# Attention and a three-way maxout layer on one core: two pairs of heads a turn, with the 64-row matmuls gathered in three stretches

## The chip, the cores and the metric

The kernel runs on one core of a Trainium2 chip. The metric is device time of one execution in microseconds (us). The kernel before takes 367.74 us, the median of three runs (367.64 to 367.95).

A core has engines that run side by side and wait for each other by semaphores. TensorE multiplies matrices; the profile calls it PE, and its weight loads PEld. VectorE is DVE, ScalarE is ACT, GpSimd is POOL. SyncE, called SP, here only issues DMAs, one after another in the order of the program. Matmul results land in PSUM, which has 8 banks, each 128 partitions wide with 512 float32 numbers per partition; everything else is in SBUF.

## The reference

```python
q, k, v: (8, 12, 448, 64) float32          # batch, heads, positions, head size
scores = matmul(q, k.transpose(0, 1, 3, 2)) / sqrt(64)
m = max(scores); e = exp(scores - m)
attn = matmul(e / (sum(e) + exp(-m) + 1e-09), v)
x = attn.transpose(0, 2, 1, 3).reshape(3584, 768)
h = maximum(maximum(x @ w1, x @ w2), x @ w3)   # weights 768 x 768
out = h @ w_out                                # 3584 x 768 float32
```

The softmax has one extra term of exp(0) in its sum. The kernel leaves the maximum out of both sides, so the sum becomes the sum of exp(scores) plus 1.

## The kernel before

**Pairs.** Heads are worked on in pairs, 6 pairs per batch, 48 in all, numbered p from 0 to 47. One iteration `it` of the loop at line 452 does the scores of pair p = it and finishes pair it - 1. A pair needs these matmuls, each 448 columns long:

- `scores(p, c)`, line 235, for three blocks c of 128 keys: two matmuls on 64 rows of the array each, one per head (line 239). They stand on different halves of the array, so that both run at once. The result fills one `ps_s` buffer of two banks; there are two such buffers.
- `scores_last(p)`, line 251: the last 64 keys of both heads in one matmul on the whole array (line 255).
- `av_main(p, hh)`, line 269, for each head: three matmuls on the whole array that sum exp(scores) times v (line 273). Columns of ones beside v give the softmax sums in the same matmul.
- `av_last(p, avs)`, line 282: two 64-row matmuls, again one per head, for the last 64 keys (line 285). Each head has one bank of `ps_av`, and there are two of them.

ACT takes the exponentials (`exp_scores`, line 249, 128 x 896 elements; `exp_last`, line 265, 128 x 448). It also makes the reciprocal of the sums as exp(-ln(sum + 1)) in `reciprocals`, lines 298 and 299. DVE multiplies by it in `normalize`, line 307, once per head.

**Dense work between.** When a batch is finished, `batch_done`, line 435, puts its maxout and output work on a list. A *group* is six matmuls into one of the two `ps_u` banks and one DVE instruction that empties it: 18 *up* groups per batch (`up_group`, lines 356, 370 and 372) and 6 or 8 *output* groups (`out_group`, lines 390 and 415). Two output groups fill one `o_sb` tile, which two DMAs on SP then write to memory (line 429). There are 6 output groups (three tiles) for even batches and 8 (four tiles) for odd ones. The pool of `o_sb` tiles, line 67, has three buffers, so every tile takes the buffer of the third tile before it, and its first write waits until both DMAs of that one have landed. `group()` takes the next group off the list. An iteration calls it three to five times, and spreads what the list holds evenly over what is left of the batch, down to `LEFT` = 4.

**Getting q and k ready.** From pair 12 on (`P_DMA`) `cast_qk(p)`, line 165, turns q and k into 16 bits on DVE, into one of two buffers. `transposes(p)`, line 209, is one DMA transpose on SP into one of three `qkT` buffers. `scale_v(p)`, line 191, prepares v on POOL. `load(p, 1)`, line 83, issues six DMAs on SP for the raw q, k and v of a pair.

**The order is written out by hand.** The pools run under a manual schedule, so each engine executes its instructions in the order in which the code emits them. From pair 12 on an iteration emits:

1. `cast_qk(it + 2)`, `transposes(it + 2)` and `scale_v(it + 1)`
2. scores and exponentials of p, blocks 0 and 1
3. one group
4. `av_main` and `av_last` of the previous pair
5. block 2 and `scores_last` of p, then reciprocals of the previous pair, then the exponentials of p
6. a group, `normalize` of head 0, a group, `normalize` of head 1, more groups
7. `load(it + 5, 1)`

So TensorE goes four times in each iteration between 64-row and whole-array matmuls: into and out of the four of step 2, and into and out of a stretch made of `av_last` and block 2.

On SP an iteration is one transpose, the output DMAs of its groups, and six loads. The code itself follows.

Of the kernel before, what the change touches and what calls it, by code (L numbers as in the profile page):

```python
# [10 lines left out]
FP32 = mybir.dt.float32  # L11
# [10 lines left out]
def kernel(  # L22
# [11 lines left out]
    nc = tc.nc  # L34
# [4 lines left out]
    NB = 3  # L39
# [125 lines left out]
    def cast_qk(p):  # L165
        qt, kt, _ = raw[(p // HB) % NRAW]
        h0 = 2 * (p % HB)
        hs = slice(h0, h0 + 2)
        k6, q6 = k16[p % NK], q16[p % NK]
        if p == 0:  # L170

            nc.scalar.copy(out=k6[:, 0:NB], in_=kt[:, hs, 0:NB].rearrange("p h c d -> p c h d"))
            for eng, cs in ((nc.scalar.copy, slice(0, 2)), (nc.vector.tensor_copy, slice(2, NB + 1))):
                eng(out=q6[:, cs], in_=qt[:, hs, cs].rearrange("p h c d -> p c h d"))
        else:
            if p >= P_DMA and (p // NPAIR) % 2:

                nc.vector.tensor_copy(
                    out=q6[:, 1 : NB + 1], in_=qt[:, hs, 0:NB].rearrange("p h c d -> p c h d")
                )  # L180
                nc.vector.tensor_copy(out=q6[64:128, 0], in_=qt[0:64, hs, NB])
            else:
                nc.vector.tensor_copy(out=q6, in_=qt[:, hs].rearrange("p h c d -> p c h d"))  # L183
            nc.vector.tensor_copy(  # L184
                out=k6[:, 0:NB], in_=kt[:, hs, 0:NB].rearrange("p h c d -> p c h d")
            )
        for hh, half in enumerate(halves):
            last = nc.gpsimd if p == 0 else nc.vector
            last.tensor_copy(out=k6[half, NB, hh], in_=kt[0:64, h0 + hh, NB])  # L189
# [14 lines left out]
    def transposes(p):  # L204
        odd = (p // NPAIR) % 2
        qkT = att_pool.tile([2 * D, 1024], MMDT, tag="qkT", bufs=3)
        qkTs[p] = qkT, 0, S
        if p >= P_DMA:
            nc.sync.dma_start_transpose(
                out=qkT.rearrange("q (c p) -> q c p", p=128),  # L210
                in_=qk16[p % NK].rearrange("p c h d -> p (c h d)"),
            )
            qkTs[p] = qkT, 64 * odd, 512
            return
        trT = ps_u.tile([128, 1024], MMDT, tag="u", name="trT")


        order = (NB, 0, 1, 2) if odd else (0, 1, 2, NB)
        n0 = 0
        for c in order:  # L220
            nc.tensor.transpose(  # L221
                out=trT[:, n0 : n0 + 128], in_=q16[p % NK][:, c], identity=ident16
            )
            n0 += SL if c == NB else 128
        for c in range(NB + 1):
            nc.tensor.transpose(  # L226
                out=trT[:, S + c * 128 : S + c * 128 + 128], in_=k16[p % NK][:, c], identity=ident16
            )
        if p == 0:
            nc.vector.tensor_copy(out=qkT[:, 0 : S + 128], in_=trT[:, 0 : S + 128])  # L230
            nc.scalar.copy(out=qkT[:, S + 128 : S + 512], in_=trT[:, S + 128 : S + 512])
        else:
            nc.vector.tensor_copy(out=qkT[:, 0 : S + 512], in_=trT[:, 0 : S + 512])  # L233
# [14 lines left out]
    def exp_scores(p, c, stp):  # L248
        nc.scalar.activation(out=eT[:, p % 2, c], in_=stp[:, :, 0:S], func=AF.Exp, scale=scale)  # L249

    def scores_last(p):
# [9 lines left out]
        )  # L261
        return stl

    def exp_last(p, stl):
        nc.scalar.activation(out=eL[:, p % 2], in_=stl[:, 0, 0:S], func=AF.Exp, scale=scale)  # L265

# [182 lines left out]
    casts(0)  # L449
    transposes(0)  # L450
    keep_busy(3)
    for it in range(NP + 1):
        p = it if it < NP else None
        prev = it - 1 if it > 0 else None
        to_next = NPAIR - it % NPAIR
        n_groups = -(-max(len(queue) - LEFT, 0) // to_next) if it % NPAIR else 4
        n_groups = max(3, min(5, n_groups))

        first = {3: 1, 4: 2}.get(it)
        if first is not None:  # L460
            hs = slice(2 * first, 2 * first + 2)
            nc.vector.memset(raw[2][0][64:128, hs, NB - 1 : NB + 1, :], 0.0)
            if first == 1:
                load(NPAIR, 1, "v")
            load(NPAIR + first, 1)
        if it in (3, 4):
            load_weight(0, it - 3)
        if it in (5, 6, 8):
            load_weight((5, 6, 8).index(it) + 1)
        if it < NPAIR:  # L470

            casts(it + 1)
            for c in range(2):
                exp_scores(p, c, scores(p, c))
            if prev is None:
                keep_busy(3)
                exp_scores(p, 2, scores(p, 2))
                transposes(1)
                exp_last(p, scores_last(p))
            else:  # L480
                den, av = (ps_av.tile([128, 512], FP32, tag="av", name=n) for n in ("den", "av"))
                sums_main(prev, den, 1)
                stp = scores(p, 2)
                sums_main(prev, av, 0)
                stl = scores_last(p)
                sums_last(prev, den, 1)
                sums_last(prev, av, 0)
                exp_scores(p, 2, stp)
                exp_last(p, stl)
                rb = reciprocals_one(den)  # L490
                transposes(it + 1)
            if it < NPAIR - 1:
                keep_busy(3)
            else:

                ups = [up_open()]
                up_part(ups[0], 0, 0, 0, range(3))
                av5 = ps_s.tile([128, 2, 512], FP32, tag="s", name="av5")
                sums_main(p, av5[:, 1], 1)
                sums_main(p, av5[:, 0], 0)  # L500
                sums_last(p, av5[:, 1], 1)
                sums_last(p, av5[:, 0], 0)
                rb5 = reciprocals_one(av5[:, 1])
            if prev is not None:
                normalize_one(prev, av, rb)
            if it == NPAIR - 1:
                normalize_one(p, av5[:, 0], rb5)
                batch_done(0)
        elif it == NPAIR:
            exp_scores(p, 0, scores(p, 0))  # L510

            up_part(ups[0], 0, 0, 0, (3,))
            ups.append(up_open())
            up_part(ups[1], 0, 0, 1, range(4))
            ups.append(up_open(ps_av, "av"))
            up_part(ups[2], 0, 0, 2, range(4))
            for dc in (4, 5):
                for fc, ps in enumerate(ups):
                    up_part(ps, 0, 0, fc, (dc,))
                    if dc == 5:  # L520
                        up_close(ps, 0, 0, fc)
            del queue[0:3]
            exp_scores(p, 1, scores(p, 1))
            group()
            casts(it + 1)
            exp_scores(p, 2, scores(p, 2))
            exp_last(p, scores_last(p))
            group()
            transposes(it + 1)
            group()  # L530
        else:
            late = it + 1 < P_DMA
            if not late:

                if it + 2 < NP:
                    cast_qk(it + 2)
                    transposes(it + 2)
                if it + 1 < NP:
                    scale_v(it + 1)
            if p is not None:  # L540
                for c in range(2):
                    exp_scores(p, c, scores(p, c))
            group()
            if late:
                casts(it + 1)
            avs = [av_main(prev, hh) for hh in range(2)]
            av_last(prev, avs)
            if p is not None:
                stp = scores(p, 2)
                stl = scores_last(p)  # L550
            rb = reciprocals(prev, avs)
            if p is not None:
                exp_scores(p, 2, stp)
                exp_last(p, stl)
            if late:
                transposes(it + 1)
            group()
            normalize(prev, 0, avs, rb)
            group()
            normalize(prev, 1, avs, rb)  # L560
            if it % NPAIR == 0:
                batch_done(prev // NPAIR)
            if it + 2 == P_DMA:
                cast_qk(it + 2)
                transposes(it + 2)
            for _ in range(n_groups - 3):
                group()

        for n in range(NPAIR + HB, 2 * NPAIR) if it == NPAIR else (it + 5,):
            if it >= NPAIR and n < NP:  # L570
                load(n, 1)
    while queue:
        group()

# [29 lines left out]
```

## Time and profile before

| | |
|---|---|
| median of 3 runs | 367.74 us |
| the profiled execution | 367.07 us |
| its span, first to last instruction | 365.3 us |
| DVE busy | 243.4 us |
| ACT busy | 221.1 us |
| POOL busy | 53.6 us |
| HBM traffic over the span | 146 GB/s |

The span is what the trace covers; about 1.8 us of the execution lie around it. In the trace a row gives start, duration, engine, source line and operation, and x6 means that six equal instructions were merged into the row. Matmuls overlap: the next one starts before the last one's duration is over, so the pace is read from starts, not from durations. A row marked SPq is a DMA's issue, and the profile tells separately how long after the start of its issue the data had landed.

### The profile page before, as it was taken

How to read it: one execution, taken by the hardware profiler on the slowest of the kernel's cores; microseconds unless marked ns; L12 is line 12 of the kernel's file. 1: busy time of each engine (PE TensorE's matmuls, PEld its weight loads, DVE VectorE, ACT ScalarE, POOL GpSimd, SP SyncE). 2: the span in 40 equal slices, each digit the busy share in tenths (PEclk: the TensorE clock that was granted, in tenths of full speed). 3: DMA queues.
4: the chain of work that ended last, by engine and by line, in shares of the span. 5: the costliest groups of instructions: out<-in, count | busy, mean ns of one | idle time of the engine just before them, and what ended most of it. 6: DMA issues, size and time to landing. Idle time of an engine off the chain costs nothing.

```text
span 365.3 us, 6122 instructions
## 1 busy us (share of the span) xinstructions
PE 357.4 (98%) x2086; PEld 163.9 (45%) x2086; DVE 243.4 (67%) x521; ACT 221.1 (61%) x335; POOL 53.6 (15%) x159
## 2 busy tenths in 40 slices
PE   8999999999999999999999999999999999999995
PEld 3434444444444444444444444444444444445552
DVE  4474777876578677577657867757666776555553
ACT  4996476765666766666567666666566766651000
POOL 4263112211211211211121121121112112000000
PEclk9999999999999999999999999999999999999999
DMA  5999997668667888849764896758675673005006
GB/s 151 229 234 229 233 247 211 155 177 214 161 180 182 208 184 154 195 107 185 182 173 122 178 200 164 175 133 214 159 174 137 165 208 83 5 2 131 2 0 172
DMA packets 87951, 58.61 MB, mean 160 GB/s; under 512 B 43504, under 2 KB 84464, under 8 KB 87920
## 3 DMA queue, kind: packets, MB, share of 16 engines
q1 hardware_dynamic: 83632, 53.18, 59.7%
q0 software_dynamic: 3920, 4.72, 7.5%
q10 hardware_dynamic: 368, 0.33, 0.4%
q8 instruction: 16, 0.26, 0.3%
q14 instruction: 15, 0.12, 0.1%
HBM read 42.47 MB, written 11.01 MB: 146 GB/s over the span
## 4 chain that ended last, share of the span: by engine, by line
PE 91%; ACT 2%; DMA 2%; DVE 2%; issue 1%; SPq 0%; DVEq 0%
PE up L356 44%; PE op L390 15%; PE av L273 13%; PE stp L239 8%; PE stl L255 4%; PE av L285 3%; DMA kin<-in_k_dram 2%; PE busy L349 2%; ACT eT L249 1%; PE trT L221 1%; PE trT L226 1%; PE av L316 1%; DVE qkT L233 1%; DVE o_sb L415 0%; DVE qk L183 0%
## 5 line engine op out<-in xcount | busy, mean ns | idle before, releaser
L356 PE MATMUL up<-xT,w 128*128 128x448 f16 x864 | 175.3, 353 | 0.7 <-DVE xT L307 0.4
L249 ACT ACTIVATE eT<-stp 128x896 f16<-128x896 f32 x144 | 125.5, 910 | 53.3 <-PE stp L239 53.3
L356 PEld LDWEIGHTS <-w 128*128 128x128 f16 x864 | 81.7, 98 | 81.7 <-issue 12.5
L372 DVE TENSOR_TENSOR hT<-hT,up 128x448 f16<-128x448 f16 x96 | 59.6, 621 | 52.1 <-PE up L356 51.1
L157 POOL TENSOR_SCALAR vst<-vin 128x384 f16<-128x384 f32 x132 | 43.1, 338 | 255.2 <-issue 159.2
L298 ACT ACTIVATE lnd<-av 64x448 f32<-64x448 f32 x84 | 45.3, 539 | 49.0 <-PE av L285 48.0
L390 PE MATMUL op<-w,hT 128*128 128x384 f16 x336 | 59.3, 326 | 0.0
L273 PE MATMUL av<-eT,vst 128*128 128x448 f16 x252 | 54.5, 352 | 0.0
L307 DVE TENSOR_TENSOR xT<-av,rb 64x448 f16<-64x448 f32 x84 | 51.8, 617 | 1.4
L239 PE MATMUL stp<-qkT 64*128 64x448 f16 x288 | 44.1, 353 | 1.5 <-DVE qkT L233 0.7
L370 DVE CAST hT<-up 128x448 f16<-128x448 f32 x48 | 29.8, 624 | 22.9 <-PE up L356 22.2
L415 DVE TENSOR_SCALAR o_sb<-op 128x384 f32<-128x384 f32 (+1 forms) x56 | 30.8, 550 | 20.0 <-PE op L390 19.0
L390 PEld LDWEIGHTS <-hT 128*128 128x128 f16 x336 | 31.6, 98 | 24.7 <-issue 4.0
L273 PEld LDWEIGHTS <-vst 128*128 128x128 f16 x252 | 24.7, 98 | 22.4
L184 DVE CAST qk<-kin 128x384 f16<-128x384 f32 x47 | 25.7, 548 | 1.1 <-DMA kin<-in_k_dram 0.7
L265 ACT ACTIVATE eL<-stl 128x448 f16<-128x448 f32 x48 | 25.9, 539 | 0.0
L299 ACT ACTIVATE rb<-lnd 128x448 f32<-128x448 f32 x42 | 24.2, 576 | 1.3
L239 PEld LDWEIGHTS <-qkT 64*128 64x128 f16 x288 | 11.0, 94 | 23.2 <-issue 16.5
L419 ACT ACTIVATE o_sb<-op 128x192 f32<-128x192 f32 x1 | 0.3, 331 | 30.2 <-DVE o_sb L415 30.2
L189 DVE CAST qk<-kin 64x64 f16<-64x64 f32 x94 | 17.5, 187 | 1.3
L255 PE MATMUL stl<-qkT 128*128 128x448 f16 x48 | 17.4, 362 | 0.0
L285 PE MATMUL av<-eL,vst 64*128 64x448 f16 x84 | 15.2, 359 | 0.0
(50 smaller groups left out, 117.7 us busy)
## 6 DMA issues: line engine op xcount, KB each, us to landing
out_dram<-o_sb SPq DMA_DIRECT2D x54, 192.0 KB, 2.8
qin<-in_q_dram SPq DMA_DIRECT2D x46, 128.0 KB, 3.0
kin<-in_k_dram SPq DMA_DIRECT2D x45, 128.0 KB, 2.9
vin<-in_v_dram SPq DMA_DIRECT2D x44, 128.0 KB, 2.9
kin<-in_k_dram SPq DMA_DIRECT2D x46, 96.0 KB, 2.7
qin<-in_q_dram SPq DMA_DIRECT2D x45, 96.0 KB, 2.7
vin<-in_v_dram SPq DMA_DIRECT2D x44, 96.0 KB, 2.8
w<-in_moe_w_dram POOLq DMA_DIRECT2D x2, 1152.0 KB, 17.1
```

The lines of the kernel that those rows point to most:

```text
L157: nc.gpsimd.tensor_scalar(out=out, in0=in_, scalar1=LAMBDA, scalar2=1.0, op0=ALU.mult, op1=ALU.mult)
L239: nc.tensor.matmul(out=stp[:, hh, 0:S], lhsT=qkT[hh * D : hh * D + D, k0 + c * 128 : k0 + c * 128 + 128], rhs=qkT[hh * D : hh * D + D, q0 ...
L249: nc.scalar.activation(out=eT[:, p % 2, c], in_=stp[:, :, 0:S], func=AF.Exp, scale=scale)
L255: nc.tensor.matmul(out=stl[:, 0, 0:S], lhsT=qkT[:, k0 + NB * 128 : k0 + NB * 128 + 128], rhs=qkT[:, q0 : q0 + S], start=True, stop=True,)
L273: nc.tensor.matmul(out=av[:, 0:S], lhsT=vst[:, p % VB, hh * NB + c, (1 - hh) * D : (3 - hh) * D], rhs=eT[:, p % 2, c, hh, :], start=(c == ...
L298: nc.scalar.activation(out=lnd[mine], in_=avs[hh][other, 0:S], func=AF.Ln, bias=1.0)
L307: nc.vector.tensor_tensor(out=xTs[b][mine, j, :], in0=avs[hh][mine, 0:S], in1=rb[mine], op=ALU.mult)
L356: nc.tensor.matmul(out=ps[:, 0:S], lhsT=w_sb[i][:, dc, ts(fc, 128)], rhs=xTs[b][:, dc, :], start=(dc == 0), stop=(dc == NDC - 1),)
L370: nc.vector.tensor_copy(out=h, in_=ps[:, 0:S])
L372: nc.vector.tensor_tensor(out=h, in0=h, in1=ps[:, 0:S], op=ALU.max)
L390: nc.tensor.matmul(out=ps[:, 0:NW], lhsT=hTs[sb][:, fc, ts(t, 128)], rhs=wout_sb[:, fc, ts(nh, NW)], start=(fc == 0), stop=(fc == NFC - 1),)
L415: nc.vector.tensor_scalar(out=o_sb[:, cs], in0=src, scalar1=1.0 / LAMBDA, scalar2=None, op0=ALU.mult)
```

## The change

The loop at line 452 now ends at pair 11. From pair 12 on a second loop does two pairs a turn, p and p + 1, in an order of its own. `av_main` of the pair before is done at the end of the previous turn. The matmuls of a turn on 64 rows stand in three stretches: `av_last` of pair p - 1 with blocks 0 and 1 of p; block 2 of p with block 0 of p + 1; `av_last` of p with blocks 1 and 2 of p + 1. The last keys of both pairs go into one two-bank buffer, and one exponential of 128 x 896 (`exp_last2`) replaces two of 128 x 448. A function `ready` casts, transposes and loads for the next turn; it is called for p + 2 after the third group and for p + 3 after the group that follows the second stretch. A turn has 8 to 10 groups.

```diff
+    def scores_last2(p):
+        stl = ps_s.tile([128, 2, 512], FP32, tag="s", name="stl")
+        for n in range(2):
+            qkT, q0, k0 = qkTs[p + n]
+            nc.tensor.matmul(
+                out=stl[:, n, 0:S],
+                lhsT=qkT[:, k0 + NB * 128 : k0 + NB * 128 + 128],
+                rhs=qkT[:, q0 : q0 + S],
+                start=True,
+                stop=True,
+            )
+        return stl
+
+    def exp_last2(stl):
+        nc.scalar.activation(out=eL, in_=stl[:, :, 0:S], func=AF.Exp, scale=scale)
...
-    for it in range(NP + 1):
-        p = it if it < NP else None
+    for it in range(P_DMA):
+        p = it
...
+    def ready(p):
+        if p < NP:
+            cast_qk(p)
+            transposes(p)
+        if p - 1 < NP:
+            scale_v(p - 1)
+        if p + 3 < NP:
+            load(p + 3, 1)
+
+    avs = [av_main(P_DMA - 1, hh) for hh in range(2)]
+    for p in range(P_DMA, NP, 2):
+        left = max(len(queue) - LEFT, 0)
+        to_next = (NPAIR - p % NPAIR) // 2
+        n_groups = 8 if p % NPAIR == 0 else max(8, min(10, -(-left // to_next)))
+        av_last(p - 1, avs)
+        stps = [scores(p, c) for c in range(2)]
+        rb = reciprocals(p - 1, avs)
+        for c in range(2):
+            exp_scores(p, c, stps[c])
+        group()
+        normalize(p - 1, 0, avs, rb)
+        group()
+        normalize(p - 1, 1, avs, rb)
+        if p % NPAIR == 0:
+            batch_done(p // NPAIR - 1)
+        group()
+        exp_last2(scores_last2(p))
+        ready(p + 2)
+        for _ in range(n_groups - 7):
+            group()
+        stps = [scores(p, 2), scores(p + 1, 0)]
+        exp_scores(p, 2, stps[0])
+        exp_scores(p + 1, 0, stps[1])
+        group()
+        ready(p + 3)
+        avs = [av_main(p, hh) for hh in range(2)]
+        av_last(p, avs)
+        stps = [scores(p + 1, c) for c in (1, 2)]
+        rb = reciprocals(p, avs)
+        for c in (1, 2):
+            exp_scores(p + 1, c, stps[c - 1])
+        group()
+        for hh in range(2):
+            normalize(p, hh, avs, rb)
+        group()
+        group()
+        avs = [av_main(p + 1, hh) for hh in range(2)]
+    av_last(NP - 1, avs)
+    rb = reciprocals(NP - 1, avs)
+    group()
+    normalize(NP - 1, 0, avs, rb)
+    group()
+    normalize(NP - 1, 1, avs, rb)
+    batch_done(B - 1)
     while queue:
         group()
```

More of the change, by code (lines that the diff above doesn't have):

```diff
@@ L533 @@
             if not late:
[L535 to L542, printed above, removed]
+                cast_qk(it + 2)
+                transposes(it + 2)
+                scale_v(it + 1)
+            for c in range(2):
+                exp_scores(p, c, scores(p, c))
             group()
@@ L547 @@
             av_last(prev, avs)
-            if p is not None:
-                stp = scores(p, 2)
-                stl = scores_last(p)
+            stp = scores(p, 2)
+            stl = scores_last(p)
             rb = reciprocals(prev, avs)
-            if p is not None:
-                exp_scores(p, 2, stp)
-                exp_last(p, stl)
+            exp_scores(p, 2, stp)
+            exp_last(p, stl)
             if late:
@@ L560 @@
             normalize(prev, 1, avs, rb)
-            if it % NPAIR == 0:
-                batch_done(prev // NPAIR)
             if it + 2 == P_DMA:
@@ L571 @@
                 load(n, 1)
+    def ready(p):
[14 more added lines that the diff above has]
+        rb = reciprocals(p - 1, avs)
+        for c in range(2):
+            exp_scores(p, c, stps[c])
[34 more added lines that the diff above has]
+    batch_done(B - 1)
     while queue:
```

## Prediction

> **What bounds the kernel now.** First the page: TensorE.
>
> ```profile
> span 365.3 us, 6122 instructions
> PE 357.4 (98%) x2086; PEld 163.9 (45%) x2086; DVE 243.4 (67%) x521; ACT 221.1 (61%) x335; POOL 53.6 (15%) x159
> PEclk9999999999999999999999999999999999999999
> PE 91%; ACT 2%; DMA 2%; DVE 2%; issue 1%; SPq 0%; DVEq 0%
> ```
>
> PE is busy nearly always at full clock and makes 91% of the chain that ended last. So either its pace changes or new waits appear on it. The timeline of PE shows the pace of one iteration (start, duration, engine, line):
>
> ```profile
> 214.27 0.55 PE L239 MATMUL stp<-qkT 64*128 64x448 f16 x4
> 214.75 1.31 PE L356 MATMUL up<-xT,w 128*128 128x448 f16 x6
> 215.90 1.30 PE L273 MATMUL av<-eT,vst 128*128 128x448 f16 x6
> 217.13 0.36 PE L285 MATMUL av<-eL,vst 64*128 64x448 f16 x2
> 217.33 0.35 PE L239 MATMUL stp<-qkT 64*128 64x448 f16 x2
> 217.61 0.36 PE L255 MATMUL stl<-qkT 128*128 128x448 f16 x1
> 217.81 3.57 PE L356 MATMUL up<-xT,w 128*128 128x448 f16 x18
> 221.31 0.36 PE L239 MATMUL stp<-qkT 64*128 64x448 f16 x2
> ```
>
> Whole-array matmuls start every 0.189 us (the chain has 18 in 3.41). Where the array changes between 64 and 128 rows more passes: 217.81 to 221.31 is 3.50, and 18 x 0.189 = 3.40; 215.90 to 217.13 is 1.23, not 1.134; two 64-row pairs take 0.48, not 0.378. Each change costs about 0.096 us, and an iteration of 7.04 us has four.
>
> Next the queue of SP:
>
> ```profile
> 173.42 1.25 SPq L209 DMA_TRANSPOSE qkT<-qk  x1
> 174.72 0.60 SPq L92 DMA_DIRECT2D qin<-in_q_dram  x1
> ...
> 178.01 0.60 SPq L93 DMA_DIRECT2D vin<-in_v_dram  x1
> 178.72 1.25 SPq L209 DMA_TRANSPOSE qkT<-qk  x1
> ```
>
> A transpose and its pair's six loads hold SP for 5.30 us (178.72 - 173.42): 1.30 and six times 0.65 with a gap, of the 7.04 that a pair lasts. Output DMAs take 0.6 us each on top, so SP has little slack. It is an in-order queue: what stands behind a late transpose is late too.
>
> **Part 1, the array changes.** Per two pairs there were eight changes, and there are six: 36 x 0.096 = 3.5 us less in 18 turns. Nothing hides this on PE. A 64-row pair that follows another costs 0.20 (217.13 to 217.33), and a stretch of three is not in the trace: its third pair costs from 0.189 to 0.20 + 0.096, as if it paid a change. The high end, twice in 18 turns, would take the 3.5 back. I take 0.20, the row of the same thing. The Trainium skill, "TensorE: Matmul & The Clock Gate", section Single matmul latency, gives a constant of 398 cycles at 2.4 GHz, an estimate of 0.163 us for an emptied array; by it 5.9 us would go. The rows above decide.
>
> **Part 2, a turn on PE, ACT and DVE.** With 0 at the end of the previous `av_main`, PE does: first stretch to 0.78 (0.096 + 0.20 + 0.20 + 0.189 + 0.096); three groups, 1.134 each for up to 4.18, 0.978 for output to 3.71; last keys 0.38; one group to 5.7 (output: 5.07); second stretch 0.58; a group, `av_main`, third stretch 0.78, three groups, `av_main`. That is 13.86 us with 8 up groups, 13.25 with four of the eight output, 14.39 with five up and four output.
> ACT starts `lnd` 0.40 after `av_last` begins (217.13 to 217.53 in the full timeline), needs 1.1 for both, 0.5 for `rb`, 0.83 for each `eT`: exponentials of blocks 0 and 1 end at 2.9 and 3.8, `exp_last2` at 5.7 or 5.2 (between 0.54, one `eL`, and 1.08, two; I take 0.91, an `eT` of the same shape). The second stretch wants its buffer for its second pair at 6.0 or 5.4: 0.2 to spare, covered by the fourth group; if it missed by as much, 18 x 0.2 = 3.6 us. `av_main` wants the third exponential 0.7 after it is there; at the turn's end 0.3 to 0.7 is left. So ACT, 0.17 us shorter per turn, costs nothing. POOL's 1.03 us of `scale_v` stays far ahead.
> DVE empties a group 0.2 after its last matmul and moves on every 0.54. Three groups and two `normalize` end at 4.9, then the first casts (1.70, row 215.21 to 216.91) at 6.6; the second end before 10.7. No bank is waited for in a turn without output tiles.
>
> **Part 3, the transposes.** Before, a transpose had two iterations, 14 us, and landed in 3.0 (median; 5.5 at most). Now the first issues at 6.65 and lands at 9.7; it is wanted at 13.9. Behind it stand six loads (from 7.95), so the second issues at 11.95 and lands at 15; `scores_last2` of the next turn wants it at 18.0. So the rest of the turn hides them with 4.2 and 3.0 us to spare; with the cover gone, each further microsecond late costs 18, one per turn. Six more loads end at 17.2, so SP runs 3.3 us into the next turn.
>
> **Part 4, the output tiles: new waits.** What is late next is the output DMA behind those loads. Odd batches have four tiles in three buffers: the fourth tile's first eviction on DVE waits for the landing of the first tile's DMAs. Played through by its rules, the list gives the first tile's two groups to the fifth and sixth of turn p = 16 (sixth and seventh of 28 and 40), and the fourth tile's first half to the third group of turns 18, 30 and 42. The first tile is written by about 11, but its two DMAs stand behind the second `load`: they issue at 17.2 and 17.8 and land 2.75 later (median 2.8), at 20.55. Turn 16 lasts 13.25, so that is 7.3 in turn 18; DVE wanted the buffer at 4.1. Behind the waiting instruction are the casts and every eviction; TensorE's fifth group wants the same `ps_u` bank at 5.65 and gets it at 7.9: 2.25 us lost. Turns 28 and 40 have nine groups, 14.39: landing at 6.16, PE at 6.75: 1.1 each. Together **4.45 us**. Before, these DMAs issued as soon as the tile was ready (gaps ahead of them in SP's timeline). The stall delays the end of the turn, so its late second transpose (16.0 in turn 18, landing 19, wanted at 19.6) just fits.
> The Trainium skill, "DMA: Bandwidth & Descriptors", section Issuing engines are not separate DMA queues, calls the sequencer's time to initiate a DMA usually small relative to the DMA. One issue is (0.60 against 2.8); fourteen in a row are not. By that rule there would be no queue and no part 4, and the sum would be rival B's.
>
> Long issues come on top:
>
> ```profile
> L209 SPq DMA_TRANSPOSE qkT<-qk x36: 1232/1255/2672, 70.1 to 308.5; - x36
> L429 SPq DMA_DIRECT2D out_dram<-o_sb x54: 466/584/2285, 77.6 to 360.0; - x54
> ```
>
> From minimum, median and maximum: now and then an issue takes 1 to 1.7 us more. In SP's timeline ten do between 68 and 300 us, one per 22, on average 0.9 more. Three paths of 11 us lead to the late tiles: 1.5 x 0.9, at least 0, at most about 5. I take 1.0.
>
> **Part 5, the entry.** `av_main` of pair 11 is pulled to the end of iteration 11, where its second bank waits for `normalize` of pair 10 (74.37 in DVE's timeline, PE ready at 73.5): 0.9. Transpose 13 lands at 79.2 (issue 76.29 + 2.9), wanted at 78.87: 0.35. Behind load 16 (until 82.9) SP issues four output DMAs (2.5), transpose 14 at 85.5, six loads, transpose 15 at 90.8, landing at 93.8, wanted at 93.1: 0.75. Sum 2.0. Gone are waits of 0.24 (73.1, transpose) and 0.54 (79.5, `xT`): 0.8. At the end of the kernel the dense work is in the same order; nothing changes.
>
> **Sum**, against the profiled execution: 367.07 - 3.5 - 0.8 + 2.0 + 4.45 + 1.0 = 370.2. The median of the runs is 0.67 above that execution, so on its scale **370.9 us**.
>
> **Rivals** (on the medians' scale).
> *A, the forecast*, 368.5 to 373: chance 0.58.
> *B, faster: the output DMAs don't hold DVE.* Then parts 1 and 5 remain: 367.74 - 3.5 - 0.8 + 2.0 = 365.4. It decides if the first tile's DMAs land before 4.1 in the next turn, 3.2 us sooner than I find for turn 18, 2.0 for the others. For it: DVE is only 67% busy and the late tile is one in seven. Against: SP's rows are regular to 0.05 us, and the order is fixed. 0.16.
> *C, even.* The entry's transposes are in time (-1.1) and no long issue falls on a path (-1.0), the stalls a fifth smaller (-0.9): 367.9. 0.11.
> *D, the transposes are late in most turns.* With landings of 6 instead of 3 us and long issues the second would miss by 0.5 in 17 turns: 379. Against: the longest of 36 is 5.5. 0.07.
> *E, the change doesn't save changes*: the third pair pays 0.096: 374.4. 0.08.
>
> Faster by over 0.2% is B, 0.16; within 0.2%, about what a measurement of this kernel can tell from no change, C, 0.11; slower A, D and E, 0.73. The range goes from B, 365.4, to E, 374.5; D and the outer edges are left out.
>
> **What would show it.** PE: 13.9 us per plain turn, its 64-row stretches 0.78, 0.58, 0.78. DVE: an `o_sb` eviction waiting 2 to 3 us for a DMA in turns 18, 30 and 42, and PE's next up group waiting for DVE. SP: output DMAs right behind loads. Wrong would be: no PE gap there (B), or PE gaps at `stl` in every turn (D).

## The result, and the profile after

The changed kernel takes 375.65 us (median of six runs, 374.46 to 376.24) against 367.74: a ratio of 1.0212, 95% interval 1.0201 to 1.0223. It is slower, as forecast, but by 7.9 us instead of 3.2, and lies just above the range. Timed again beside the experiments it took 373.52 us (371.72 to 374.68) against 367.47, a ratio of 1.0154 (1.0126 to 1.0181); its time differs more between executions than that of the kernel before.

The profiled execution took 376.17 us, 9.1 more than that of before. First its page:

```profile
span 374.4 us, 6097 instructions
...
PE 357.3 (95%) x2086; PEld 167.3 (45%) x2086; DVE 244.6 (65%) x521; ACT 220.0 (59%) x317; POOL 54.1 (14%) x159
...
PEclk9999999999999789999999999999999999999999
...
PE 74%; DMA 12%; SPq 6%; DVE 4%; issue 2%; ACT 1%; DVEq 0%
```

PE has the same 2086 matmuls and nearly the same busy time in a span 9.1 us longer. The chain that ended last now leads through DMAs and SP's queue for 18%, and in two of the 40 slices the granted clock is not whole. So the time went into waits and into a slower clock. Where no wait falls, the turn is as planned. From the timeline of PE (start, duration, line), the third stretch of a turn and the first of the next:

```profile
259.63 0.36 PE L302 MATMUL av<-eL,vst 64*128 64x448 f16 x2
259.83 0.54 PE L239 MATMUL stp<-qkT 64*128 64x448 f16 x4
260.31 3.58 PE L373 MATMUL up<-xT,w 128*128 128x448 f16 x18
263.73 1.30 PE L290 MATMUL av<-eT,vst 128*128 128x448 f16 x6
264.96 0.36 PE L302 MATMUL av<-eL,vst 64*128 64x448 f16 x2
```

259.63 to 260.31 is 0.68, and 0.096 stand ahead of it: the 0.78 of the prediction. Turns without waits last 13.88, 13.24 or 14.40 us (13.86, 13.25, 14.39 forecast). Two iterations of the kernel before took 0.21 us more for the same groups, so 18 turns save 3.8.

The waits of the changed kernel (who waited for whom, total, times, longest):

```profile
DVE o_sb L432 <- DMA out_dram<-o_sb: 8.4, 3, 3.7
...
PE up L373 <- DVE o_sb L432: 6.0, 3, 2.9
...
PEld L269 <- DMA qkT<-qk: 3.3, 5, 0.8
```

Three times DVE waits for an output tile's DMA before it may write `o_sb`, and each time PE then waits for DVE. The timelines of DVE (one row) and PE show the first, in turn 18:

```profile
127.07 0.56 DVE L432 TENSOR_SCALAR o_sb<-op 128x384 f32<-128x384 f32 x1 [3.67 <-DMA out_dram<-o_sb]
```

```profile
124.27 0.55 PE L239 MATMUL stp<-qkT 64*128 64x448 f16 x4
127.68 2.40 PE L373 MATMUL up<-xT,w 128*128 128x448 f16 x6 [2.86 <-DVE o_sb L432]
129.87 2.45 PE L290 MATMUL av<-eT,vst 128*128 128x448 f16 x6
```

The four matmuls of the second stretch take 0.48 from start to the next, so the up group comes 2.9 us late. The other two times, in turns 30 and 42, it is 1.7 and 1.5. And in turn 18 the six matmuls of the group then take 2.2 us instead of 1.13. The table by stretches tells why (the clock is the column before the DMA share):

```profile
124.50:127.70 3.20, 0.34 (x5) 0.11 (x2) 0.60 (x2) 1.73 (x2) 0.00 (x0) 0.87 0.89 268
127.70:133.70 6.00, 6.00 (x19) 2.02 (x19) 4.27 (x12) 0.83 (x2) 0.95 (x3) 0.50 0.55 151
```

For 6 us after the wait the clock is half. From 127.68 PE needs 9.29 us for what takes 6.47 in turn 24: another 2.8 us. What held DVE is seen in SP's queue:

```profile
117.62 1.25 SPq L209 DMA_TRANSPOSE qkT<-qk  x1
...
121.57 1.16 SPq L92 DMA_DIRECT2D vin<-in_v_dram  x1
122.77 0.60 SPq L93 DMA_DIRECT2D vin<-in_v_dram  x1
123.47 3.75 SPq L446 DMA_DIRECT2D out_dram<-o_sb  x6
```

The first tile is complete at 116.8 (on DVE the eviction of its second half starts at 116.23 and takes 0.56). Its two DMAs issue at 123.47 and 124.07, behind a transpose and six loads, one of them a long issue; they land at 126.95, and DVE writes at 127.07.

### The profile page after: what moved, and what is told of

Its sections match the earlier page's. It is cut to its first block, busy times and chain, and to the rows that moved or that the text cites. A ratio compares the mean times of both kernels' runs of the same rounds, so it can differ in the third digit from the quotient of the medians.

```text
span 374.4 us, 6097 instructions
## 1 busy us (share of the span) xinstructions
PE 357.3 (95%) x2086; PEld 167.3 (45%) x2086; DVE 244.6 (65%) x521; ACT 220.0 (59%) x317; POOL 54.1 (14%) x159
## 4 chain that ended last, share of the span: by engine, by line
PE 74%; DMA 12%; SPq 6%; DVE 4%; issue 2%; ACT 1%; DVEq 0%
PE up L373 39%; PE av L290 12%; PE op L407 10%; PE stp L239 6%; DMA qkT<-qk 6%; DMA kin<-in_k_dram 4%; PE av L302 3%; SPq L92 3%; SPq L93 2%; DMA out_dram<-o_sb 2%; PE stl L269 1%; DVE o_sb L432 1%; DVE xT L324 1%; ACT eT L249 1%; DVE hT L389 0%
## 5 line engine op out<-in xcount | busy, mean ns | idle before, releaser
L249 ACT ACTIVATE eT<-stp 128x896 f16<-128x896 f32 x144 | 123.6, 909 | 23.1 <-PE stp L239 23.1
L290 PE MATMUL av<-eT,vst 128*128 128x448 f16 x252 | 55.8, 358 | 0.6 <-DVE xT L324 0.6
L239 PE MATMUL stp<-qkT 64*128 64x448 f16 x288 | 41.2, 355 | 2.0 <-DVE qkT L233 0.7
L279 ACT ACTIVATE eL<-stl 128x896 f16<-128x896 f32 x18 | 16.5, 917 | 16.9 <-PE stl L269 16.9
L239 PEld LDWEIGHTS <-qkT 64*128 64x128 f16 x288 | 12.7, 95 | 20.1 <-issue 11.9
L189 DVE CAST qk<-kin 64x64 f16<-64x64 f32 x94 | 20.6, 219 | 1.0
L183 DVE CAST qk<-qin 128x512 f16<-128x512 f32 x29 | 12.9, 446 | 0.2
```

What stands on the lines that cost most here:

```text
L239: nc.tensor.matmul(out=stp[:, hh, 0:S], lhsT=qkT[hh * D : hh * D + D, k0 + c * 128 : k0 + c * 128 + 128], rhs=qkT[hh * D : hh * D + D, q0 ...
L290: nc.tensor.matmul(out=av[:, 0:S], lhsT=vst[:, p % VB, hh * NB + c, (1 - hh) * D : (3 - hh) * D], rhs=eT[:, p % 2, c, hh, :], start=(c == ...
```

## The experiments

All ran beside the kernel before, which took 367.47 to 367.62 us each time. Theory 1: the fourth output tile of odd batches waits for DMAs that stand behind loads on SP, and this makes the loss. Rivals: the transposes, with half the lead, make it (2); the saved array changes save nothing (3). What a wait costs is given, here and below, as the time that PE loses against the same place of a turn without the wait; the expectations, which count the change of the array as well, have the same waits 0.1 us longer.

**The changed kernel again.** 

> The changed kernel once more, unaltered, for a second trace. Theory 1 (the fourth output tile of an odd batch waits for DMAs that stand behind loads on SP): the three PE waits in turns 18, 30 and 42 come back at 3.0, 1.8 and 1.6 us within 0.8, and hold most of the loss in this execution too. Rival (late transposes or other waits that differ from run to run make the loss): the three waits are smaller and other places larger. Time 374 to 376.5 by both.

372.64 us, a single execution, less than the 374 to 376.5 expected. The three waits cost 2.7, 1.5 and 1.4 us, and there is no half clock before the end of the kernel. They come back at the same places and sum to 5.6, more than the 5.1 us lost here, which is net of the saving. But 2.5 us of late transposes are there too, at the last keys of turns 12, 14 and 32 and at the first stretch of turn 14.

**Four output tiles.**

```diff
-    out_pool = ctx.enter_context(tc.tile_pool(name="outp", bufs=3))
+    out_pool = ctx.enter_context(tc.tile_pool(name="outp", bufs=4))
```

> The changed kernel with four output tiles in the pool instead of three, nothing else. Theory 1: the fourth tile no longer waits, so the waits of 3.0, 1.8 and 1.6 us go, and with the first of them the 6.8 us of half clock (3.0 us lost): 375.65 - 9.5 = 366.2, 366 to 368 as some transposes stay late. Rival 2 (the transposes of the next turn are late because their lead was halved): 373 or more, the PE waits at the last-keys matmul remain and grow. Rival 3 (six array changes a turn save nothing against eight): 369.5 to 371.

368.82 us, ratio 1.0034 (1.0023 to 1.0046). The line DVE <- DMA is gone from the waits and turns 18, 30 and 42 last 13.24, so theory 1 holds for 3.8 us or more (372.64 less 368.82). It isn't all: the time misses the expected 366 to 368, for the other line grew:

```profile
PEld L269 <- DMA qkT<-qk: 5.0, 6, 1.5
```

Without the stall, the transposes behind it have less time: 0.95 us are lost at the last keys of turn 20 and 1.21 at those of turn 32, where they were late by 0 to 0.6 before. Rival 2 is part of the answer.

**The second load at the end of the turn, three tiles.** `ready(p, False)` is `ready` without its load.

```diff
-        ready(p + 3)
+        ready(p + 3, False)
...
         avs = [av_main(p + 1, hh) for hh in range(2)]
+        if p + 6 < NP:
+            load(p + 6, 1)
```

> The changed kernel with three output tiles as it was, but the second load of a turn issued at the turn's end, behind the output DMAs instead of ahead of them. Theory 1 (it is the place in the queue): the first tile's DMAs issue 4 us sooner and land at about 3.4 of the next turn, before the fourth tile wants the buffer at 4.1: 366 to 368, the same as with four buffers. If three buffers are too few whatever the order on SP: 373 or more.

369.19 us (ten runs, 367.13 to 371.36), ratio 1.0048 (1.0023 to 1.0074). Turns 18, 30 and 42 are 13.24 again, with three tiles: it is the place in the queue that made the wait, not the number of tiles alone. The time misses for the same reason as before: the second transpose of turn 18 is issued late behind the output DMAs and the loads, and PE waits 2.4 us at the last keys of turn 20.

**Eight changes instead of six, four tiles.**

```diff
-        stps = [scores(p, 2), scores(p + 1, 0)]
-        exp_scores(p, 2, stps[0])
-        exp_scores(p + 1, 0, stps[1])
+        exp_scores(p, 2, scores(p, 2))
         group()
+        exp_scores(p + 1, 0, scores(p + 1, 0))
```

> Four output tiles as in the run of that name, and the second stretch split again: block 0 of the second pair comes a group later, so a turn has eight changes between 64-row and whole-array matmuls instead of six; no work is added or left out. If a change costs 0.096 us: 18 x 0.19 = 3.5 us more than with four buffers alone. If the changes cost nothing net (rival 3): within 0.5 us of it.

370.74 us, 1.9 more than with six. The median is between the two expectations, but the turns are clear: each free of waits is 0.21 longer (13.45 for 13.24, 15.22 for 15.01). The longer turns gave late transposes time, which hid the rest; the last run below takes that away.

**The changed kernel, timed.** 

> The changed kernel unaltered, timed on the same chip as the runs beside it, so that they can be compared with it. 372 to 376.5 us; the waits of turns 18, 30 and 42 again 1.5 to 3 us each. Where the wait of turn 18 stays under about 3 us and the granted clock stays whole, 372 to 374; where the clock halves behind it, 375 to 376.5.

373.52 us. The waits cost 2.7, 1.7 and 1.6 us, and the clock is half from 126.8 to 130.2.

**Both transposes ahead of both loads, four tiles.**

```diff
-        ready(p + 2)
+        ready(p + 2, False)
...
-        ready(p + 3)
+        ready(p + 3, False)
+        for n in (p + 5, p + 6):
+            if n < NP:
+                load(n, 1)
```

> Four output tiles as in that run, and both transposes of a turn ahead of both loads on SP; no work is added or left out. Theory (what is left after four tiles is late transposes at the last-keys matmul, 0.9 to 1.2 us in turns 20 and 32 and more in some executions): these waits go, the second transpose lands about 2 us sooner, 366 to 367.5 us. If those waits come from something else, or if loads that come later make the casts wait: 368.5 or more.

367.32 us, ratio 0.9996 (0.9987 to 1.0004), as expected. The waits at the last keys of turns 20 and 32 are gone. A new one of 1.0 us is in turn 20's first stretch: with twelve loads and six output DMAs in a row on SP the first transpose of turn 18 starts at 128.75.

**The entry as well.**

```diff
                 scale_v(it + 1)
+                load(it + 4, 1)
...
             normalize(prev, 0, avs, rb)
-            group()
-            normalize(prev, 1, avs, rb)
+            if late:
+                group()
+                normalize(prev, 1, avs, rb)
+            else:
+                normalize(prev, 1, avs, rb)
+                group()
...
-            if it >= NPAIR and n < NP:
+            if NPAIR <= it < P_DMA - 2:
...
-        for n in (p + 5, p + 6):
+        for n in ((p + 4,) if p == P_DMA else ()) + (p + 5, p + 6):
```

> The same, and the entry mended: the loads of pairs 15 and 16 stand behind the transposes of 13 and 15, and in iteration 11 the second normalize comes ahead of the group's eviction. Theory: the waits of the entry (0.7 at av_main of pair 11, 0.6 at the last keys of turn 12, 0.6 at those of turn 14, 0.4 at turn 14's end) go as well: 2 us less than with the transposes first, 364 to 366, faster than the kernel before by 0.5 to 1%. If six changes instead of eight are worth nothing: 367.5 or more.

365.44 us, ratio 0.9954 (0.9941 to 0.9967): faster than the kernel before. The four waits of the entry are gone but for 0.1 us; turns 12 and 14 last 13.40 and 15.01.

**Two output tiles.**

```diff
-    out_pool = ctx.enter_context(tc.tile_pool(name="outp", bufs=3))
+    out_pool = ctx.enter_context(tc.tile_pool(name="outp", bufs=2))
```

> The changed kernel with two output tiles instead of three, nothing else: the suspected wait made longer. By the same sums the third tile of an odd batch waits for the first: PE loses about 5.1 us in turn 18 and 4.0 in turns 30 and 42 (2.8, 1.6 and 1.5 with three), and about 1.7 in turns 24 and 36, where none was. Those over 3 us let the granted clock halve for 3 to 7 us, 1.5 to 3 us more each: 385 to 395. If it isn't the wait for the buffer: 372 to 378.

394.17 us, ratio 1.0729 (1.0696 to 1.0762). The waits and, from PE's timeline, the longest:

```profile
DVE o_sb L432 <- DMA out_dram<-o_sb: 31.8, 7, 9.0
...
PE op L407 <- DVE o_sb L432: 16.0, 4, 6.7
```

```profile
121.68 1.30 PE L407 MATMUL op<-w,hT 128*128 128x384 f16 x7
129.65 1.76 PE L407 MATMUL op<-w,hT 128*128 128x384 f16 x5 [6.67 <-DVE o_sb L432]
```

PE loses 6.8, 4.4 and 4.6 us in turns 18, 30 and 42 (5.1, 4.0, 4.0 expected), 1.9 in turns 24 and 36 (1.7), and 2.3 in turn 12, which the sums had not. The clock is half for 6.8, 3.4 and 6.8 us behind the three longest.

**v by GpSimd, three tiles.**

```diff
-            load(p + 3, 1)
+            load(p + 3, 1, "qk")
+            load(p + 3, 1, "v", (nc.gpsimd, nc.gpsimd))
```

> The changed kernel with three output tiles and its own order, and only the loads of v taken off SP to GpSimd's queue. Theory (SP's two blocks of loads hold the first output tile's DMAs): they issue 2.6 us sooner, land at 4.7 instead of 7.3 of turn 18 and before 4.1 in turns 30 and 42, so the three waits of 2.8, 1.8 and 1.7 us go down to 0 to 0.5, without a fourth tile: 366 to 368.5, against 372 to 376. If three tiles are simply too few, or if the wait is for the transfer and not for the queue: 371 or more.

367.64 us (ten runs, 366.90 to 370.61), ratio 1.0017 (0.9994 to 1.0039). With 2.6 us of issue off SP turns 30 and 42 have no wait at three tiles, where the bound was thus SP's time to issue. In turn 18 a wait of 1.2 stays: the first tile's second DMA issues about 3 us sooner, but takes 4.4 us to land instead of 2.9. Of the edits that change one thing in the changed kernel this one brings most back, and it moves no work on PE, DVE or ACT.

**Dummy matmuls in the wait of turn 18.**

```diff
+        if p == 18:
+            ps = ps_s.tile([128, 2, 512], FP32, tag="s", name="fill")
+            for _ in range(6):
+                nc.tensor.matmul(
+                    out=ps[:, 0, 0:S], lhsT=idle[:, 0:128], rhs=idle, start=True, stop=True
+                )
```

> The changed kernel with six dummy matmuls, whose result nothing reads, in the wait of turn 18 ahead of the group that waits; they add work and take none away. The wait itself stays (from the end of the second stretch to the group's first matmul 2.8 to 3 us). If the half clock comes from an idle PE, it is gone in every execution: 371.5 to 373, granted clock 0.998 or more. If it comes from something else, it is seen as often as without them (0.988 to 0.995 in most executions) and the time is 372 to 376.

372.96 us (372.64 to 374.15), mean granted clock 1.000 in three executions and 0.995 in the slowest; without them it was 0.995, 0.994, 0.998 and 1.000. Four executions of each don't settle what halves the clock, and one went against the expectation. The traces say more, for each records when the granted clock changes. In the changed kernel's first trace it falls at 126.84, returns at 133.66 and falls again at 372.60, after the last matmuls. With two tiles it changes at 125.68, 132.51, 221.25, 224.67, 310.00, 316.83 and 388.50. The distances in the second list are 2, 26, 1, 25, 2 and 21 times 3.413 us, and those in the first 2 and 70 times. In all fourteen traces of this case the changes lie on such a grid, whose start differs from execution to execution. So the clock is decided at the ends of stretches of 3.413 us. Here they are around the wait of turn 18, in the changed kernel's first trace, its second, and the one with dummy matmuls (length, PE busy, and the clock ahead of the DMA share):

```profile
123.42:126.84 3.42, 1.40 (x10) 0.63 (x9) 0.00 (x0) 2.62 (x3) 0.00 (x0) 1.00 0.81 232
126.84:130.25 3.41, 2.57 (x8) 1.02 (x8) 2.85 (x8) 0.00 (x0) 0.00 (x0) 0.50 0.54 182
130.25:133.66 3.41, 3.41 (x13) 1.02 (x12) 2.01 (x6) 0.79 (x2) 0.95 (x3) 0.50 0.61 148
133.66:137.08 3.42, 3.42 (x19) 1.76 (x18) 2.12 (x4) 2.47 (x4) 0.00 (x0) 1.00 0.74 201
```

```profile
123.29:126.70 3.41, 1.86 (x13) 0.88 (x11) 0.44 (x1) 2.62 (x3) 0.00 (x0) 1.00 0.77 215
126.70:130.11 3.41, 2.30 (x12) 1.07 (x11) 2.81 (x8) 0.03 (x1) 0.00 (x0) 1.00 0.62 202
```

```profile
125.86:129.27 3.41, 1.72 (x9) 0.81 (x9) 1.00 (x2) 1.07 (x2) 0.00 (x0) 1.00 0.92 263
129.27:132.69 3.42, 3.42 (x22) 1.49 (x21) 3.32 (x10) 1.06 (x2) 0.95 (x3) 1.00 0.59 169
```

The length less PE's busy time is PE's idle time. In the first trace one stretch has 2.02 us of it, and the clock is half from its end. In the second trace a wait of nearly the same length falls across a boundary, as 1.55 and 1.11, and the clock stays whole. In the third the up group comes 3.6 us late, more than in any other trace with three tiles, but the dummy matmuls leave no stretch with more than 1.69 idle, and the clock stays whole. Over all fourteen traces, every stretch with 2.02 us or more idle, in the middle of a kernel or at its end, is followed by half clock as far as the trace goes, and none with 1.84 or less is. So the half clock comes from idle PE, and where the wait falls between the boundaries decides whether it comes. The slowest execution with dummy matmuls has no trace, and its 0.995 stays open.

**Everything together: v by GpSimd, four tiles, transposes first, entry mended.**

> The version with four output tiles, transposes first and the entry mended, and from pair 17 on the loads of v issued on GpSimd's queue instead of SP's, which takes 2.6 us of issue per turn from SP. If SP's queue is still what makes the last late transposes (1.0 us in turn 20), that wait goes: 364 to 365.2 us. If GpSimd's descriptors slow something down (its own scale_v, or DVE at the casts): 365.5 or more.

363.8 us, a little under the 364 to 365.2 expected, ratio 0.9894 (0.9879 to 0.9908): 3.8 us less than the kernel before beside it, and 9.7 less than the 373.52 of the changed one. No wait of a tile or transpose is left on PE:

```profile
span 362.0 us, 6058 instructions
...
PE 354.3 (98%) x2086; PEld 167.7 (46%) x2086; DVE 244.4 (68%) x521; ACT 220.0 (61%) x317; POOL 92.6 (26%) x223
...
PEclk9999999999999999999999999999999999999999
```

POOL is busy 38.5 us longer than in the changed kernel: 64 issues of 0.6 us. It has the time.

**The same with eight changes.** The edit of the other run with eight, on this version. 

> The fastest version (four output tiles, transposes first, entry mended, v by GpSimd) with the second stretch split, so that a turn has eight changes between 64-row and whole-array matmuls instead of six; no work is added or left out. The first such test moved the time by 1.9 us and each turn by 0.21, because the longer turns also gave late transposes time. Here no transpose is late: 18 x 0.21 = 3.8 us more than 363.8, 367.2 to 368, that is the time of the kernel before. If the changes are worth less than the turns show: 364 to 366.5.

368.3 us, 4.5 more than with six (3.8 expected): all of the gain goes. The two timelines of the middle of a plain turn, six changes first:

```profile
258.83 2.43 PE L373 MATMUL up<-xT,w 128*128 128x448 f16 x12
261.20 0.55 PE L239 MATMUL stp<-qkT 64*128 64x448 f16 x4
261.68 1.31 PE L373 MATMUL up<-xT,w 128*128 128x448 f16 x6
262.83 1.30 PE L290 MATMUL av<-eT,vst 128*128 128x448 f16 x6
```

```profile
262.08 2.43 PE L373 MATMUL up<-xT,w 128*128 128x448 f16 x12
264.44 0.36 PE L239 MATMUL stp<-qkT 64*128 64x448 f16 x2
264.74 1.31 PE L373 MATMUL up<-xT,w 128*128 128x448 f16 x6
265.98 0.36 PE L239 MATMUL stp<-qkT 64*128 64x448 f16 x2
```

The split pair takes 0.30 in one place (264.44 to 264.74) and its partner as much later, with a change of 0.096 ahead of each: 0.79. Together in a stretch the two take 0.48 (261.20 to 261.68) and one change ahead, 0.58. 18 times 0.21 is 3.8; the other 0.7 are mostly in turns 16, 28 and 40, 0.4 longer instead of 0.2. Rival 3 is refuted.

## Why the prediction was right or wrong

It was right that the kernel gets slower, and right about where and by what chain of waits. Two steps of the sum failed. It has no term for PE's clock behind the waits that it forecasts: it counts on at full clock, and half clock cost 2.8 us in the profiled execution. And "Together **4.45 us**" was too small: the three waits cost 6.2. The sum of the profiled execution, term by term (us):

| step | forecast | measured |
|---|---|---|
| 1, array changes | -3.5 | -3.8 |
| waits of before that go | -0.8 | -0.8 |
| 5, entry | +2.0 | +2.4 |
| 4, output tiles, with long issues | +5.45 | +6.2 |
| half clock behind the first | none | +2.8 |
| other late transposes and small waits | none | +1.7 |
| ahead of the first changed line | none | +0.5 |
| sum (of unrounded terms) | +3.15 | +9.1 |

The 0.5 is no effect of the change: iteration 11 begins at 67.95 us instead of 67.44, and up to there both kernels have the same code.

*Part 1* held: 0.096 us per change, and the third pair of a stretch costs 0.20. The estimate from the Trainium skill's page "TensorE: Matmul & The Clock Gate", section Single matmul latency (398 cycles at 2.4 GHz are 0.166, not 0.163, so 6.0 for 36 changes), is too high here; the runs with eight changes show 0.21 for two.

*Part 2* held for ACT and nearly for DVE: in turn 16 the first output group waits 0.35 us for `hT`, since the casts stand ahead of the eviction that writes it. "No bank is waited for in a turn without output tiles" is still right; this wait is for data.

*Part 3* failed in "with 4.2 and 3.0 us to spare". That was worked out for a plain turn. With output DMAs ahead of a transpose the 3.0 are used up: turns 26, 32 and 44 lose 0.48, 0.37 and 0.24, the first of them also by a transpose whose issue took 2.41 instead of 1.25. Part 4's late second transpose "just fits" behind turn 18, as forecast (turn 20 lasts 13.88), but not behind turns 30 and 42.

*Part 4* had the right mechanism, tiles, turns and order, and three executions show it at the places named. Its size was off: the waits cost 2.93, 1.73 and 1.54 us, forecast as 2.25, 1.1 and 1.1. Each time the transposes issued 0.15 later than worked out, the second output DMA took 2.8 to 3.0 to land instead of 2.75, and DVE and PE followed 0.1 to 0.2 later. In turn 16 a long issue in the path took 0.55 more, and the turn itself lasted 0.35 longer, which took that much back. Of the 1.75 us that were missing, the 1.0 for long issues covers more than half in the sum, but only one of the three paths had such an issue: that part of the fit is luck.

The sum left out altogether what a wait of 3 us does to PE's clock. Half clock cost nearly as much as the wait itself. The Trainium skill, "TensorE: Matmul & The Clock Gate", Part 1: The HAM clock gate, says that an idle window of about 3.4 us lets the clock fall to half, and that the windows run freely. The traces agree on the windows, with boundaries 3.413 us apart whose place differs from execution to execution. They differ on the idle time: no window had to be idle as a whole, 2.02 us of it were enough. So waits of 2.68, 2.73 and 2.93 us in turn 18 gave 3.4, 0 and 6.8 us of half clock, and the forecast wait of 2.25 was already long enough for it to be possible.

*Part 5* came within 0.4, in part by luck: `av_main` and the last keys of turn 14 lost 0.73 and 0.47 instead of 0.9 and 0.75, and the first stretch of turn 14 lost 0.70 that the sum had not. The rivals: B's condition, that DVE is not held, was brought about by four tiles and by the load at the turn's end, and for two turns of three by v on GpSimd. These gave 367.6 to 369.2 and not 365.4, because late transposes stayed. D, as a rival that stands alone, is wrong, but a small form of it is in three of the plain turns behind output tiles (26, 32 and 44, but not 20 and 38). The rule on issue time that part 4 quotes from the Trainium skill, "DMA: Bandwidth & Descriptors", section Issuing engines are not separate DMA queues, does not fit this queue: taking 2.6 us of issue per turn off SP brought the time from 373.5 to 367.6.

## What to carry to other kernels

An in-order DMA queue that is busy for three quarters of the time is a resource like an engine: when a reordering puts a block of loads ahead of a store, work out when the store lands and who reuses its buffer. A saving on the busiest engine is safe only after the slack of every transfer has been worked out for the worst turn, not the plain one. And a wait of 2 to 3 us on TensorE should be priced at up to twice its length.

## What the runs showed of the hardware

- A change between 64-row and whole-array matmuls costs 0.096 us, and a 64-row pair behind another 0.20 instead of 0.189, in stretches of two and of three pairs.
- The granted clock changed only at boundaries 3.413 us apart, whose place differed from execution to execution. It went to 0.50 behind every such stretch with 2.02 us or more of idle PE and behind none with 1.84 or less. In the middle of a kernel it came back after one or two stretches: behind those with at most 0.56 us idle, not behind those with 0.84 or more.
- Loads issued on GpSimd's queue took 0.6 us each there, as on SP, and in the run with everything together landed in 3.5 us instead of 2.8; there SP's output DMAs landed later as well, in 3.6 instead of 3.0.
